# Opened steps: an output product between A11 and A12 instead of behind both

## The chip, the cores and the metric

The kernel runs on one core of one Trainium2 chip. The metric is the device time of one launch in microseconds (us); less is better. Times of several runs are given as their median.

The engines go by the names that the profile uses: PE is TensorE (PEld its weight loads, which overlap its matmuls), DVE is VectorE, ACT is ScalarE, POOL is GpSimd, SP is the queue that issues most transfers. PSUM is the memory that matmuls write to, in banks of 512 fp32 columns for each of 128 partitions.

## What is computed

Two blocks in a row, all in fp32: a filter in the frequency domain along the sequence, and then an MLP with SiLU on every token.

```python
# x (8, 3008, 256); filt_r, filt_i (1505, 256)
X = np.fft.rfft(x, axis=1)
Y = X * (filt_r + 1j * filt_i)[None]
y = np.fft.irfft(Y, n=3008, axis=1).astype(np.float32)
# w_in (256, 2048); w_out (2048, 256); 24064 tokens
h = y.reshape(24064, 256) @ w_in
g = h * (1.0 / (1.0 + np.exp(-h)))
out = g @ w_out
```

## The kernel before

**The MLP as a run of steps.** The 3008 tokens of a batch are taken as two halves of the channel-major tile `y`, and each half in three pieces, so that a batch has six "pairs" (a pair is two token blocks of 256, or of 240 in the last piece of a half). The 2048 hidden channels are eight blocks of 2 x 128. A step is one pair with one such block, so a batch has 48 steps (`STEPS`) and the kernel 384. In each step the 2 x 2 block product with w_in is done with seven products instead of eight (combinations of weights named A11, A12, S3, A22, S1, S2, S4 and sums of tokens in `ty`), and the product with w_out likewise, with seven output products.

**`hidden(step)`, line 719**, computes the hidden half of a step. It is a generator; between two `yield`s lies one round, and there are eight rounds. Two PSUM banks take its products: `px` (tag `x`) for A11, S2, S3 and A22, which accumulate on each other, and `pyz` (tag `yz`), whose first 256 columns are `yo` (S1, S4) and whose second 256 are `zo` (A12). In order:

- round 0: A11 into `px`; ScalarE copies it to `sums[:, 0]` (line 740)
- round 1: A12 into `zo`; VectorE adds the copy to it and writes g0 (line 743); then `finish()` lets VectorE do the last two sums of the step before, g6 and g7 (lines 770 and 771)
- round 2: S2 onto `px`; ScalarE copies it (747) and applies SiLU to g0
- round 3: S1 into `yo`
- round 4: S3 onto `px`; ScalarE copies it (753), VectorE adds it to `yo` for g2 (754)
- round 5: nothing
- round 6: A22 onto `px`; ScalarE takes SiLU from it (g3), then SiLU of g2
- round 7: S4 onto `yo`; VectorE's sum g1 (762), SiLU of it, and the sums g4 and g5 (764)

**`project(step)`, line 778**, is the other generator: the seven output products of a step, one to a round, each reading one of g0 to g7 and adding to one of four accumulator banks. In the order of `PROJECT` (line 775) they read g0, g3, g2, g4, g5, g6, g7; at the first step of a pair the order is another. Here they are called p1 to p7. `LAG` is 1: while `hidden(step)` runs, `project(step - 1)` runs.

**The loop, line 1141,** interleaves the two by hand: every engine executes its instructions in the order in which they are written out here. In each of `ROUNDS` = 8 rounds it lets `hidden` and then `project` go on by one, and then `until` writes out whatever is due from the plan (`pending`): the pieces of the Fourier stages for the next batches, the token sums of the next pair, the output's transposes and stores.

**Opened steps.** Some pieces of the Fourier stages have to borrow the banks `x` and `yz`, which only stand free between two steps. Where such pieces are planned, `open_step` (line 658) puts the step into the set `opened` and plans the pieces 0.06 of a step ahead of it. In an opened step the loop first writes out two output products (line 1149 to 1151), then the borrowed pieces (line 1152), then the eight rounds. Since two output products are used up, `project` has five left and is held back in two rounds (line 1154). `plan(b, ...)` opens three steps for each batch b from 2 on and two for batch 1, counted from the batch's first step:

- 44 steps ahead (not for batch 1): `stage1` of rows 6, with its two results in `x` and `yz`, evicted by ScalarE (`x`) and VectorE (`yz`), and then `stage1` of rows 7 in banks of its own
- 36 steps ahead: `stage3` of the batch before in `x` and `yz`, evicted by VectorE (`x`) and ScalarE (`yz`), and then `forward` of group 0 in banks of its own
- 10 steps ahead: `stage3` of groups 0 (in `x` and `yz`) and 1 (own banks); in this step's round 1 the token sums of a later pair (`tokens`, line 709) are also written out, three operations of VectorE

Of the kernel before, what the change touches and what calls it, by code (L numbers as in the profile page):

```python
# [167 lines left out]
def kernel(  # L168
# [421 lines left out]
    joined, opened = set(), set()  # L590
# [176 lines left out]
    def finish():  # L767

        for g, n in unfinished:
            combine(v, g[:, 6, 0:n], g[:, 2, 0:n], g[:, 4, 0:n], ALU.subtract)  # L770
            combine(v, g[:, 7, 0:n], g[:, 3, 0:n], g[:, 6, 0:n], ALU.subtract)
        unfinished.clear()
# [5 lines left out]
    def project(step):  # L778

        pair, jp = divmod(step, NJP)  # L780
        n, g = pairs[pair][3], g_t.pop(step)
        if jp == 0:
            acc[pair] = {}
        last = jp == NJP - 1

        order = PROJECT
        if jp == 0 and step in joined:
            order = PROJECT[0:2] + PROJECT[3:5] + PROJECT[2:3] + PROJECT[5:]
        elif jp == 0:
            order = PROJECT[2:3] + PROJECT[0:2] + PROJECT[3:]  # L790
        for c, k, i, h in order:
            if i not in acc[pair]:
                acc[pair][i] = accps.tile([128, 2, 256], FP32, name=f"acc_{pair}_{i}", tag=f"a{i}")

            nc.tensor.matmul(out=acc[pair][i][:, h, 0:n], lhsT=w_t[:, jp, c, 1], rhs=g[:, k, 0:n],  # L795
                             start=(jp == 0 and h == 0), stop=last, skip_group_check=True)
            if last and (h == 1 or i == 3):
                drain(pair, i)
            yield
# [327 lines left out]
    for pair in range(len(pairs)):  # L1127
        step, rnd = combines[pair % per] if pair != 1 else (7, 5)
        pending.append((pair // per * STEPS + step + rnd / ROUNDS, 98, lambda pair=pair: tokens(pair)))
        for chunk in range(2 if pair < len(pairs) - 1 else 0):  # L1130
            step, rnd = stores[pair % per][chunk]
# [4 lines left out]
    def until(time):  # L1136
        while pending and pending[0][0] <= time:
            pending.pop(0)[2]()

    until(-1e-3)  # L1140
    for step in range(n_steps + LAG):
        work = []
        if step < n_steps:
            work.append(hidden(step))
        else:
            finish()
        if step >= LAG:
            work.append(project(step - LAG))
        if step in opened:
            for _ in range(2):  # L1150
                next(work[1])
        until(step - 0.05)
        for rnd in range(ROUNDS):
            held = work[1:] if step in opened and rnd in (0, 2) else []
            work = [w for w in work if w in held or next(w, work) is not work]
            until(step + rnd / ROUNDS)
        assert not work
# [30 lines left out]
```

## Time and profile before

| what | value |
|---|---|
| median of 3 runs | 2586.41 us (2585.56 to 2587.24) |
| profiled execution | 2588.03 us, of which the span from first to last instruction 2586.3 us |
| granted TensorE clock | 0.995 |
| output products (L795), matmuls | 5376, 1508.7 us busy, 375 ns each |
| products into `px` from `ty` (L732) | 2304, 678.1 us busy, 376 ns each |
| products into `pyz` from `y` (L732) | 1536, 454.2 us busy, 377 ns each |
| VectorE sums out of `pyz` (L703) | 1152, 479.7 us busy, 416 ns each |

The page's busy times are unions by group: two matmuls overlap in the pipeline, so one that is shown with 375 ns starts 0.215 us after the one before it. Every fp32 product is two such matmuls (x2 in a row of the timeline), so a product of 256 tokens takes 0.43 us of TensorE. All sums of VectorE, whatever the line that asks for them, carry the line of their helper `combine`, L703; they are told apart by their tiles: `g<-pyz,abc` is a sum out of the bank, `g<-g` one of the others, `ty<-y` a token sum.

In rows of the order of time the first number is the start in us from the start of the span, the second the length; x2 means that two instructions of one kind were merged; brackets give the idle time of the engine ahead of the row and the instruction that ended it. A row of waits has the waiting instruction, the one that it waited for, the sum in us, how often, and the longest.

### The profile page before, as it was taken

The page shows a single profiled execution, that of the slowest core. Times are in us where ns is not written, and L with a number is a line of the kernel's source. Part 1 is how long each engine was busy: PE and PEld are TensorE (multiplying, and loading weights), DVE is VectorE, ACT ScalarE, POOL GpSimd, SP SyncE. Part 2 cuts the span into 40 slices and gives each one's busy share as a digit, 9 for nine tenths or more (in the row PEclk, how much of TensorE's full clock was granted, in tenths as well). Part 3 has the DMA queues.
Part 4 walks back from the last instruction along what each step waited for, and adds up shares of the span by engine and source line. Part 5 has one row for each costly group of instructions (what it writes and reads, how often), then busy time and mean ns, then how long its engine had stood idle before and what let it go on. Part 6 is the DMA issues. An engine that isn't in the chain of part 4 may idle for free.

```text
span 2586.3 us, 48366 instructions
## 1 busy us (share of the span) xinstructions
PE 2560.6 (99%) x18972; PEld 2198.1 (85%) x18972; DVE 1681.0 (65%) x3569; ACT 1113.9 (43%) x3014; POOL 424.9 (16%) x672
## 2 busy tenths in 40 slices
PE   8999999999999999999999999999999999999998
PEld 6688888888888888888888888888888888888987
DVE  7766666666666766666666666666666676555554
ACT  3544444444444444444444444444444444444443
POOL 2211211121112111211122111211121112101101
PEclk9899999999999999999999999999999999999999
DMA  8431232212222222231223222331232211210000
GB/s 276 142 90 45 68 83 67 60 53 82 63 63 64 71 65 58 70 78 59 68 51 89 58 66 58 79 76 52 64 74 67 73 45 27 65 20 16 9 17 17
DMA packets 200077, 171.08 MB, mean 66 GB/s; under 512 B 122116, under 2 KB 174196, under 8 KB 199060
## 3 DMA queue, kind: packets, MB, share of 16 engines
q1 hardware_dynamic: 178520, 117.04, 19.0%
q0 software_dynamic: 16928, 44.65, 5.4%
q10 hardware_dynamic: 4400, 6.29, 0.8%
q8 instruction: 149, 2.44, 0.4%
q14 instruction: 80, 0.66, 0.1%
HBM read 96.05 MB, written 81.26 MB: 69 GB/s over the span
## 4 chain that ended last, share of the span: by engine, by line
PE 95%; DVE 2%; DMA 1%; ACT 1%; issue 0%; ACTq 0%; SPq 0%; DVEq 0%
PE acc L795 43%; PE px L732 25%; PE pyz L732 19%; PE pd L560 3%; PE pb L446 2%; PE pc L489 2%; PE pf L416 1%; DMA w_t<-in_x_dram 0%; DVE g L703 0%; PE pa L342 0%; DMA filt<-in_filt_r_dram 0%; DMA d_t<-d_tbl 0%; PE pa L333 0%; DMA raw<-in_moe_w_out_dram 0%; ACT t L349 0%
## 5 line engine op out<-in xcount | busy, mean ns | idle before, releaser
L795 PE MATMUL acc<-g,w_t 128*128 128x256 f32 (+1 forms) x5376 | 1508.7, 375 | 0.4 <-DVE g L703 0.4
L795 PEld LDWEIGHTS acc<-g,w_t 128*128 128x128 f32 x5376 | 1021.3, 190 | 115.6 <-DVE g L703 0.8
L703 DVE TENSOR_TENSOR g<-pyz,abc 128x256 f32<-128x256 f32 (+1 forms) x1152 | 479.7, 416 | 614.9 <-ACT abc L753 360.1
L703 DVE TENSOR_TENSOR g<-g 128x256 f32<-128x256 f32 (+3 forms) x1152 | 599.3, 520 | 196.9 <-ACT g L736 183.7
L732 PE MATMUL px<-ty,w_t 128*128 128x256 f32 (+1 forms) x2304 | 678.1, 376 | 0.5 <-ACT abc L753 0.5
L736 ACT ACTIVATE g<-g 128x256 f32<-128x256 f32 (+1 forms) x1152 | 472.9, 410 | 250.1 <-DVE g L703 250.1
L703 POOL TENSOR_TENSOR s<-s 128x256 f32<-128x256 f32 (+1 forms) x329 | 255.1, 793 | 1412.7 <-DVE s L815 1307.6
L732 PEld LDWEIGHTS px<-ty,w_t 128*128 128x128 f32 x2304 | 432.3, 190 | 64.5 <-issue 8.2
L732 PE MATMUL pyz<-y,w_t 128*128 128x256 f32 (+1 forms) x1536 | 454.2, 377 | 0.0
L732 PEld LDWEIGHTS pyz<-y,w_t 128*128 128x128 f32 x1536 | 283.4, 189 | 48.3 <-DVE g L703 8.6
L747 ACT COPY abc<-px 128x256 f32<-128x256 f32 (+1 forms) x384 | 141.5, 368 | 364.6 <-PE px L732 364.6
L753 ACT COPY abc<-px 128x256 f32<-128x256 f32 (+1 forms) x384 | 141.9, 370 | 336.1 <-PE px L732 335.3
L736 ACT ACTIVATE g<-px 128x256 f32<-128x256 f32 (+1 forms) x384 | 146.1, 381 | 297.3 <-PE px L732 297.2
L732 PE MATMUL px<-y,w_t 128*128 128x256 f32 (+1 forms) x768 | 232.2, 384 | 2.0 <-ACT y L246 1.0
L732 PE MATMUL pyz<-ty,w_t 128*128 128x256 f32 (+1 forms) x768 | 225.7, 376 | 0.2 <-DVE g L703 0.2
L732 PEld LDWEIGHTS px<-y,w_t 128*128 128x128 f32 x768 | 140.3, 189 | 34.9 <-DVE y L582 5.8
L732 PEld LDWEIGHTS pyz<-ty,w_t 128*128 128x128 f32 x768 | 144.5, 190 | 18.8 <-DVE g L703 1.0
L740 ACT COPY abc<-px 128x256 f32<-128x256 f32 (+1 forms) x384 | 135.8, 354 | 45.0 <-PE px L732 45.0
L560 PEld LDWEIGHTS pd<-wi_t,t 48*64 48x64 f32 x4096 | 67.2, 138 | 30.9 <-ACT g L736 16.4
L560 PE MATMUL pd<-wi_t,t 48*64 48x47 f32 x4096 | 73.5, 236 | 5.7 <-issue 3.5
L428 POOL DMA_DIRECT2D d<-tf x144 | 71.7, 505 | 31.3 <-DVE tf L424 27.3
L815 ACT COPY s<-acc 128x512 f32<-128x512 f32 (+1 forms) x94 | 54.3, 578 | 47.5 <-PE acc L795 47.4
(118 smaller groups left out, 1312.7 us busy)
## 6 DMA issues: line engine op xcount, KB each, us to landing
t<-d SPq DMA_DIRECT2D x120, 192.0 KB
d<-q POOLq DMA_DIRECT2D x86, 256.0 KB, 2.6
t<-d SPq DMA_DIRECT2D x84, 256.0 KB
out_dram<-o SPq DMA_DIRECT2D x636, 32.0 KB
d<-tf POOLq DMA_DIRECT2D x144, 96.0 KB, 3.5
xr<-in_x_dram SPq DMA_DIRECT2D x6, 1472.0 KB
x_all<-in_x_dram SPq DMA_DIRECT2D x72, 96.0 KB
x_all<-xr SPq DMA_DIRECT2D x72, 96.0 KB
```

What stands on the lines that cost most here:

```text
L428: nc.gpsimd.dma_start(out=d1[k // 2, :, k % 2, n0:n0 + 4], in_=us["tf"][32 * k:32 * k + NS].rearrange("p q n c -> p (q n) c"))
L446: nc.tensor.matmul(out=ps[k][32 * j:32 * j + 32, ri, :], lhsT=d_t[rows, 4 * g + at, ri, :], rhs=t2[rows, at, :], start=True, stop=True)
L489: nc.tensor.matmul(out=ps[j][64 * k:64 * k + 64, a, :], lhsT=e_t[rows, g + a, k, ri, :], rhs=zs[k][rows, ri, :], start=(a == 0 and ri == 0 ...
L560: nc.tensor.matmul(out=ps[h][c0:c0 + 64, cb, i, :], lhsT=t4s[g][rows, i, 128 * cb + c0:128 * cb + c0 + 64], rhs=wi_t[rows, :], start=True, ...
L703: eng.tensor_tensor(out=out, in0=in0, in1=in1, op=op)
L732: nc.tensor.matmul(out=out, lhsT=w_t[:, jp, c, 0], rhs=rhs, start=start, stop=True, skip_group_check=True)
L736: nc.scalar.activation(out=g[:, k, 0:n], in_=g[:, k, 0:n] if src is None else src, func=AFT.Silu)
L740: nc.scalar.copy(out=sums[:, 0, 0:n], in_=xo)
L747: nc.scalar.copy(out=sums[:, 1, 0:n], in_=xo)
L753: nc.scalar.copy(out=sums[:, 2, 0:n], in_=xo)
L795: nc.tensor.matmul(out=acc[pair][i][:, h, 0:n], lhsT=w_t[:, jp, c, 1], rhs=g[:, k, 0:n], start=(jp == 0 and h == 0), stop=last, skip_group ...
L815: copy(out=s[:, 2 * i:2 * i + 2, 0:n], in_=acc[pair][i][:, :, 0:n])
```

## The change

One line of the loop. In an opened step `project` is held in rounds 1 and 2 and no longer in rounds 0 and 2:

```diff
         until(step - 0.05)
         for rnd in range(ROUNDS):
-            held = work[1:] if step in opened and rnd in (0, 2) else []
+            held = work[1:] if step in opened and rnd in (1, 2) else []
             work = [w for w in work if w in held or next(w, work) is not work]
             until(step + rnd / ROUNDS)
```

The order of products in an opened step, after p1, p2 and the borrowed pieces:

```
before: A11 A12 p3  S2 S1 p4 S3 p5 p6 A22 p7 S4
after:  A11 p3  A12 S2 S1 p4 S3 p5 p6 A22 p7 S4
```

With A12 its sum g0 and the sums of `finish()` are written out one product later. The other 364 steps are as they were.

## The prediction

> **What bounds the kernel now.** I read the page's busy shares first, then the chain of waits, then the waits of the weight loads, then the order of time in single steps. Products are named by the weight combination that they use: a step computes A11, A12, S2, S1, S3, A22, S4 (w_in), and the output products p1 to p7 of the step before stand among them.
>
> The page's busy row and the first line of its chain:
> ```profile
> PE 2560.6 (99%) x18972; PEld 2198.1 (85%) x18972; DVE 1681.0 (65%) x3569; ACT 1113.9 (43%) x3014; POOL 424.9 (16%) x672
> ...
> PE 95%; DVE 2%; DMA 1%; ACT 1%; issue 0%; ACTq 0%; SPq 0%; DVEq 0%
> ```
> TensorE is the bound: a moment in which it stands still in the main loop lengthens the span by as much, and the other engines matter only as far as a product waits for them. So the question is what waits the new order makes.
>
> From the waits of the weight loads:
> ```profile
> PEld pyz L732 <- DVE g L703: 9.7, 34, 0.6
> ```
> Products of the pyz bank already wait 34 times, 9.7 us in all, for VectorE sums that read that bank. Such a wait is the one to look for.
>
> One opened step, engine by engine (start, length; a stage-3 and a forward block stand before it, and its p1 and p2 before those). TensorE:
> ```profile
> 489.65 0.70 PE L732 MATMUL px<-y,w_t 128*128 128x256 f32 x2
> 490.18 0.59 PE L732 MATMUL pyz<-y,w_t 128*128 128x256 f32 x2
> 490.61 0.59 PE L795 MATMUL acc<-g,w_t 128*128 128x256 f32 x2
> 491.05 0.59 PE L732 MATMUL px<-ty,w_t 128*128 128x256 f32 x2
> 491.48 0.59 PE L732 MATMUL pyz<-ty,w_t 128*128 128x256 f32 x2
> ```
> VectorE in the same stretch:
> ```profile
> 490.88 0.42 DVE L703 TENSOR_TENSOR g<-pyz,abc 128x256 f32<-128x256 f32 x1 [1.31 <-ACT abc L740]
> 491.22 0.87 DVE L703 TENSOR_TENSOR g<-g 128x256 f32<-128x256 f32 x2
> ```
> And the weight loads of S1 and p4:
> ```profile
> 491.36 0.31 PEld L732 LDWEIGHTS pyz<-ty,w_t 128*128 128x128 f32 x2
> 491.69 0.41 PEld L795 LDWEIGHTS acc<-g,w_t 128*128 128x128 f32 x2
> ```
> The matmul rows are A11, A12, p3, S2, S1: one product each 0.43 us (490.18, 490.61, 491.05, 491.48). Only A11 to A12 takes 0.53, as TensorE restarts after the block. The first VectorE row is g0, the sum at line 743 that reads A12's half of the pyz bank. S1's weight load starts at 491.36, 0.06 after g0 ends (490.88 + 0.42 = 491.30), and S1 writes the other half of that bank. The other two kinds of opened step show the same: g0 ends 438.30 and S1's load starts 438.35; 348.45 and 348.51. Three equal distances: I take it that S1 waits for g0. Now it costs nothing: S1's matmul still starts 0.43 after S2's.
>
> An ordinary step with a product between A11 and A12, for the time from A12 to g0:
> ```profile
> 469.32 0.59 PE L732 MATMUL pyz<-y,w_t 128*128 128x256 f32 x2
> ...
> 470.02 0.42 DVE L703 TENSOR_TENSOR g<-pyz,abc 128x256 f32<-128x256 f32 x1 [0.75 <-PE pyz L732]
> ```
> g0 starts 0.70 after A12's first matmul (0.11 after the modelled end) and ends at 470.44. There S1 comes four products after A12 (471.05), so nothing shows.
>
> VectorE's work in the kind of opened step that carries a pair's token differences:
> ```profile
> 348.03 0.42 DVE L703 TENSOR_TENSOR g<-pyz,abc 128x256 f32<-128x256 f32 x1 [1.28 <-ACT abc L740]
> 348.37 0.88 DVE L703 TENSOR_TENSOR g<-g 128x256 f32<-128x256 f32 x2
> 349.17 0.65 DVE L703 TENSOR_TENSOR ty<-y 128x480 f32<-128x480 f32 x1
> 349.85 0.85 DVE L703 TENSOR_TENSOR ty<-y,ty 128x240 f32<-128x240 f32 x2
> 350.62 0.80 DVE L582 COPY y<-pd 128x376 f32<-128x376 f32 x1
> 351.26 0.42 DVE L703 TENSOR_TENSOR g<-pyz,abc 128x256 f32<-128x256 f32 x1
> ```
> The weight load of S4 there:
> ```profile
> 351.73 0.30 PEld L732 LDWEIGHTS pyz<-y,w_t 128*128 128x128 f32 x2 [0.31 <-DVE g L703]
> ```
> From g0 on VectorE is not idle for 3.6 us; S4 then waits 0.31 for the last sum. So whatever delays g0 also delays S4.
>
> **What the Trainium skill says.** "PSUM — Partial Sum Buffer", section "PSUM bank collisions raise a hardware error": access by two engines has to be kept apart by bank and quadrant, not by address; disjoint columns of one bank still collide. That is why S1 (columns 0 to 255 of the bank) must stay behind a sum that reads columns 256 to 511, and the 0.05 to 0.06 us in three steps agree. Same page, "Engine vs sequencer instructions": matmuls start in program order and VectorE's queue is first in, first out; so p4 and all behind it wait with S1, and everything behind g0 moves with g0. The trace agrees: p4's load is the next after S1's. "Perfetto Trace Analysis", "Tensor Engine Instruction (MATMUL, LD_WEIGHTS)": the shown end of a matmul is an estimate and its semaphore comes later; the 0.11 us from A12's end to g0 is that, so I use start-to-start times.
>
> **The change part by part.** Opened steps are counted from the plan: batch 1 has two (36 and 10 steps ahead of the batch), batches 2 to 7 have three (44, 36, 10), 2 + 6 x 3 = 20 of 384. All have 256 tokens, and the step projected in them is never a pair's first, so p3 is always S4 with g2.
>
> Removed and added instructions: none. No DMA, no copy and no issue on SP's or POOL's queue is moved; two products change places on TensorE, and with A12 its sum g0 and the two sums of the unfinished step (line 769) come later on VectorE.
>
> *p3 earlier by one place.* It reads g2, whose Silu ended before the block (433.42 to 433.83 in the step whose A11 starts at 436.64). Cost 0, gain 0, because TensorE is kept busy either way.
>
> *A11 to S2.* Between them stand two products as before, so ScalarE's copy of A11 (490.44 to 490.81) stays hidden: 0.
>
> *A12 later by one place.* Its matmul starts at 490.61 and not 490.18. Could that take away a wait of A12 for its bank? Its bank's eviction by ScalarE ended at 489.61, before A11; the 0.53 is the restart and is paid by whichever product follows A11. Bounds: 0 to -0.10 a step; I take 0.
>
> *g0 and S1.* Before, g0 started with the later of ScalarE's copy (490.81) and A12. Now A12 decides: 490.61 + 0.70 = 491.31, end 491.73, S1's load 491.79, its matmul 0.12 later at 491.91, where it was 491.48. TensorE stands for 0.43 us, since only S2 is left between A12 and S1. Queued behind S1 are p4, S3, p5, p6, A22, p7 and S4, and ScalarE's copy of S3 and the sum g2 wait for S3: the rest of the step moves as a whole. Bounds: counting from g0's start in the three kinds (0.43 to 0.45 later) gives at most 0.45; counting to the matmul after S1 (a product that follows an idle restart starts 0.54 after the load, as A12 after A11: 491.79 + 0.54 = 492.33, where p4 was 491.91) gives 0.42. I take 0.43, ends 0.41 and 0.45.
>
> *What follows.* The unfinished sums end 0.43 later, and p6 needs the first of them (g6): g0's end + 0.44. S1's load + four products (1.7 us) is where p6 loads. No wait. ScalarE's Silu of g0 starts at 491.95, behind the copy of S2 (from 491.68), and g0's new end, 491.73, is ahead of that: 0. In the seven steps 10 ahead of a batch VectorE's row is 0.43 later as a whole, but S4 is 0.43 later too, so the 0.31 stays 0.31 and isn't paid twice.
>
> Sum: 20 x 0.43 = 8.6 us (8.2 to 9.0). Against the profiled execution: 2588.03 us (span 2586.3 and 1.7 around it) becomes 2596.6. That execution lies 1.6 above the median of the runs, 2586.41, to which the same sum gives 2595.0.
>
> **The rivals.**
> *S1 doesn't wait for g0.* Then the 0.06 is chance, and only the seven token steps lose, as g0's delay reaches S4: 7 x 0.43 = 3.0 us, 2589.4. For it: the two halves are different data. Against: three equal distances, and the bank rule. Chance 0.06.
>
> *The stall is absorbed (the other side: not slower).* Later in the loop TensorE waits anyway, for example at the pyz loads (9.7 us in all). If those waits end on work that the delay doesn't touch, the 0.43 is taken out of them; it decides from the point where the waits in the two steps after reach 0.43. With all of it absorbed and A12's restart gain of up to 0.10: 2586.4 down to 2584.4. For it: VectorE is idle 35% of the span. Against: no weight load in two of the three kinds waits in the rest of its step, and in the third the wait begins with g0 itself. Chance 0.05.
>
> *The token steps pay twice.* If S4's wait grows by the delay on top of S1's: 8.6 + 7 x 0.43 = 11.6 us, 2598.0. For it: VectorE's unbroken row. Against: both ends of that wait move alike. Chance 0.07.
>
> **How the numbers follow.** My forecast has 0.82: 2595.0. What can be told from no change is about 0.2%, 5.2 us. Slower: 0.82 + 0.07 = 0.89. Within: 0.06 + 0.03 of the absorbed case = 0.09. Faster 0.02. The range is the forecast's 8.2 to 9.0 with some 2 us for medians of few runs below, and up to the double payment: 2592.0 to 2598.2; 0.11 lies below it.
>
> **What would show it.** In the changed kernel the weight load of S1 in the 20 opened steps carries a wait for VectorE's g, some 0.5 us from the end of S2's load; the row "pyz waits for g" grows from 34 times to about 54, and from 9.7 by about 10 us. g0 starts 0.70 after A12 and names PE as releaser, not ScalarE. S4's 0.31 in the token steps stays. I am wrong if S1's load comes ahead of g0's end, or if the steps after an opened one lose waits that they have now.

## The result and the profile after

| | median | runs | ratio to before (95% interval) |
|---|---|---|---|
| before | 2586.74 us | 6 | |
| after | 2595.76 us | 6 | 1.0036 (1.0023 to 1.0048) |

The change makes the kernel slower: the ratio is 1.0036, and the medians lie 9.0 us apart. The profiled executions have spans of 2586.3 and 2594.4 us.

The busy row and the first row of the chain, of the changed kernel:

```profile
PE 2564.0 (99%) x18972; PEld 2196.5 (85%) x18972; DVE 1682.0 (65%) x3569; ACT 1113.2 (43%) x3014; POOL 424.0 (16%) x672
...
PE 94%; DVE 3%; DMA 1%; ACT 1%; issue 1%; POOL 0%; DVEq 0%; SPq 0%; ACTq 0%; POOLq 0%
```

The instruction counts are those of before. In the chain VectorE's share has gone from 2 to 3% and TensorE's from 95 to 94% (rounded; the whole loss is under 0.4%): there are more places where TensorE stands until VectorE lets it go on. The waits of the weight loads say which (the pyz row had 9.7 us in 34 waits before):

```profile
PEld pyz L732 <- DVE g L703: 21.6, 59, 0.6
```

The opened step that the prediction took apart, in the changed kernel; it starts 1.03 us later now. TensorE's matmuls are A11, p3, A12, S2, S1:

```profile
490.68 0.70 PE L732 MATMUL px<-y,w_t 128*128 128x256 f32 x2
491.22 0.59 PE L795 MATMUL acc<-g,w_t 128*128 128x256 f32 x2
491.65 0.59 PE L732 MATMUL pyz<-y,w_t 128*128 128x256 f32 x2
492.08 0.59 PE L732 MATMUL px<-ty,w_t 128*128 128x256 f32 x2
492.83 0.70 PE L732 MATMUL pyz<-ty,w_t 128*128 128x256 f32 x2 [0.15 <-DVE g L703]
```

VectorE, from g0 on:

```profile
492.35 0.42 DVE L703 TENSOR_TENSOR g<-pyz,abc 128x256 f32<-128x256 f32 x1 [1.74 <-PE pyz L732]
492.69 0.87 DVE L703 TENSOR_TENSOR g<-g 128x256 f32<-128x256 f32 x2
```

And the weight loads of S2 and S1:

```profile
491.89 0.38 PEld L732 LDWEIGHTS px<-ty,w_t 128*128 128x128 f32 x2
492.83 0.30 PEld L732 LDWEIGHTS pyz<-ty,w_t 128*128 128x128 f32 x2 [0.56 <-DVE g L703]
```

g0 starts 0.70 after A12 and names TensorE as what it waited for, where it had named ScalarE's copy. (In the kernel before it also started 0.70 after A12, 490.18 to 490.88, though the view names the copy there.) It ends at 492.77, and S1's load starts 0.06 later, after an idle time that the view now puts down to VectorE's g. From A11 to S1's load it is 2.15 us; before it was 1.72. The matmul row names only 0.15 us of idle time, since the modelled end of S2 reaches far into the gap. The loss is read better from the loads, or from the starts: S1's matmul starts 0.75 after S2's, where it was 0.43, and the product behind it another 0.54 later, where it was 0.43. The first gives 0.32 us, the second 0.11.

In a token step (an opened step with the token sums, 10 steps ahead of a batch) S4 waits as before (0.31 then):

```profile
352.34 0.30 PEld L732 LDWEIGHTS pyz<-y,w_t 128*128 128x128 f32 x2 [0.33 <-DVE g L703]
```

The whole loss can be read without modelled ends, from A11 of one opened step to A11 of the next. These are starts of A11's weight load in the order of time, subtracted, for one batch; each stretch belongs to the opened step at its head. Of all 19 stretches 17 are longer by 0.41 to 0.45 us. The other two, behind the token steps at 659 and 1286 us in the kernel before, differ by -0.04 and +0.57. Each holds a long wait of TensorE in or just behind a stage-3 block that varies from profile to profile: 1.06 us at 681 us became 0.57 (put down to no instruction), and 0.96 us at 1307 us became 1.09 (for the block's eviction).

| kernel | from the token step (10 ahead) | from the step 44 ahead | from the step 36 ahead |
|---|---|---|---|
| before | 89.82 | 53.00 | 169.72 |
| after | 90.26 | 53.43 | 170.14 |
| after less before | 0.44 | 0.43 | 0.42 |

The same starts taken from one step to the next leave those waits out. From A11 of an opened step to A11 of the step behind it, each of the 20 is longer by 0.42 to 0.45 us, 8.5 us in all; of the other steps only three differ by more than 0.06 us (the very first, and the two with the waits just named). So every opened step costs 0.42 to 0.45 us, whatever pieces it has borrowed the banks for, and the sum lies inside the interval of the measured ratio (6 to 12 us).

### The profile page after: what moved, and what is told of

It reads as the page before. It is cut to its first block, busy times and chain, and to the rows that moved or that the text cites. A ratio compares the mean times of both kernels' runs of the same rounds, so it can differ in the third digit from the quotient of the medians.

```text
span 2594.4 us, 48366 instructions
## 1 busy us (share of the span) xinstructions
PE 2564.0 (99%) x18972; PEld 2196.5 (85%) x18972; DVE 1682.0 (65%) x3569; ACT 1113.2 (43%) x3014; POOL 424.0 (16%) x672
## 4 chain that ended last, share of the span: by engine, by line
PE 94%; DVE 3%; DMA 1%; ACT 1%; issue 1%; POOL 0%; DVEq 0%; SPq 0%; ACTq 0%; POOLq 0%
PE acc L795 43%; PE px L732 25%; PE pyz L732 19%; PE pd L560 3%; PE pb L446 2%; PE pc L489 2%; DVE g L703 1%; PE pf L416 1%; DMA x_all<-in_x_dram 1%; DVE w_t L302 1%; PE pa L342 0%; DMA raw<-in_moe_w_out_dram 0%; DVE w_t L703 0%; ACT t L349 0%; DVE p L468 0%
```

## The experiments

The theory is that of the prediction: S1 writes the bank from which VectorE reads g0, so it waits for that read; with A12 one product later only S2 is left to hide it. The rivals are that a late A12 costs by itself, that the wait is for something else, and that part of the cost lies in VectorE's long row in the token steps. All times are medians, beside runs of the kernel before on the same chip: 2586.12 us for the first four, 2585.45 us for the last two.

### A12 late, S1 a product later

```diff
-            held = work[1:] if step in opened and rnd in (0, 2) else []
+            held = work[1:] if step in opened and rnd in (1, 3) else []
```

> Opened steps run A11 p3 A12 S2 p4 S1 S3: A12 is as late as in the changed kernel, but two products (S2 and p4) stand between A12 and S1 again. Theory (S1 waits for g0, the reader of its bank): no wait of S1 in any of the 20 steps; g0 starts 0.43 us later than before, which only reaches S4 in the seven token steps, where its wait grows from 0.31 to about 0.74: 7 x 0.43 = 3.0 us over the kernel before, ratio 1.0012. Rival (a late A12 is what costs, wherever S1 stands): as the changed kernel, about 9 us, ratio 1.0035.

Measured: 2588.96 us, ratio 1.0011 (1.0004 to 1.0018); the rival's 1.0035 is outside. The weight loads from S2 to S1 in the step of 36 ahead (rows: S2, p4, S1), and g0 there:

```profile
490.54 0.38 PEld L732 LDWEIGHTS px<-ty,w_t 128*128 128x128 f32 x2
490.94 0.41 PEld L795 LDWEIGHTS acc<-g,w_t 128*128 128x128 f32 x2
491.47 0.31 PEld L732 LDWEIGHTS pyz<-ty,w_t 128*128 128x128 f32 x2
```
```profile
490.99 0.42 DVE L703 TENSOR_TENSOR g<-pyz,abc 128x256 f32<-128x256 f32 x1 [1.73 <-PE pyz L732]
```

g0 is as late as after the change, and S1's load still starts 0.06 behind its end (491.41). But p4 has filled the time, and nothing is lost. S4 of the token step pays in its place:

```profile
351.42 0.30 PEld L732 LDWEIGHTS pyz<-y,w_t 128*128 128x128 f32 x2 [0.73 <-DVE g L703]
```

The 0.31 has become 0.73. By stretches: 90.25, 53.00, 169.72. Only the token steps lose, 0.43 to 0.44 each from step to step; the other 13 opened steps run as before with a late A12. What counts is the distance from A12 to S1.

### Nothing reads the bank

```diff
-            held = work[1:] if step in opened and rnd in (0, 2) else []
+            held = work[1:] if step in opened and rnd in (1, 2) else []
...
-        combine(v, g[:, 0, 0:n], zo, sums[:, 0, 0:n], ALU.add)
+        combine(v, g[:, 0, 0:n], sums[:, 0, 0:n] if step in opened else zo, sums[:, 0, 0:n], ALU.add)
```

> The changed order, but in the 20 opened steps the sum g0 reads ScalarE's copy twice and not A12's half of the bank (left out: A12's product in g0 of these steps), so that nothing reads the bank between A12 and S1. Theory: S1 no longer waits, g0 starts with ScalarE's copy as before, S4's 0.31 in the token steps stays: time of the kernel before, ratio 1.0000 within 0.0007. Rival (the place of A12 or p3 on TensorE itself costs, or the wait is for something other than the read): about 8 to 9 us, ratio 1.0033.

Measured: 2584.95 us, ratio 0.9997 (0.9989 to 1.0005); the rival's 1.0033 is outside. This kernel leaves A12's product out of g0 in the opened steps, and nothing else. The changed order, with the same products in the same places, costs nothing when g0 doesn't read A12's half. g0, and the loads of S2 and S1:

```profile
487.94 0.43 DVE L703 TENSOR_TENSOR g<-abc 128x256 f32<-128x256 f32 x1 [1.26 <-ACT abc L740]
```
```profile
487.96 0.38 PEld L732 LDWEIGHTS px<-ty,w_t 128*128 128x128 f32 x2
488.36 0.41 PEld L732 LDWEIGHTS pyz<-ty,w_t 128*128 128x128 f32 x2
```

S1's load starts 0.02 after S2's ends, and just before g0 (487.94 to 488.37) has ended; g0 itself no longer waits for A12. In the six steps 44 ahead of a batch g0 ends 0.05 before S1's load, so the times alone could not tell a wait from chance there. The instructions in the traces can: in the kernel before and in the changed one S1's load carries a wait for the semaphore that VectorE's sums count up, in all 384 steps; in this kernel it carries none in the 20 opened steps, and still does in the other 364. Stretches: 89.80, 53.01, 169.71, the kernel before.

### The bank is read twice, in the order of before

```diff
-        combine(v, g[:, 0, 0:n], zo, sums[:, 0, 0:n], ALU.add)
+        for _ in range(2 if step in opened else 1):
+            combine(v, g[:, 0, 0:n], zo, sums[:, 0, 0:n], ALU.add)
```

> The order of before, but in the 20 opened steps VectorE makes the sum g0 twice, one after the other, so that the bank is read 0.34 to 0.42 us longer (start to start of two such sums, and the length of one). Theory: S1, which stood just behind g0 without losing time, now waits 0.34 to 0.42: 20 x 0.34 to 0.42 = 6.8 to 8.4 us, ratio 1.0026 to 1.0032. Rival (S1 doesn't wait for the read; only VectorE's longer row in the token steps reaches S4): 7 x 0.34 = 2.4 us, ratio 1.0009.

Measured: 2594.62 us, ratio 1.0033 (1.0020 to 1.0045); the rival's 1.0009 is outside. A12 stands where it stood before and S1 stalls all the same. The two sums, and S1's load:

```profile
491.40 0.89 DVE L703 TENSOR_TENSOR g<-pyz,abc 128x256 f32<-128x256 f32 x2 [1.31 <-ACT abc L740]
```
```profile
492.34 0.30 PEld L732 LDWEIGHTS pyz<-ty,w_t 128*128 128x128 f32 x2 [0.58 <-DVE g L703]
```

The second read ends at 492.29, S1's load starts 0.05 later. The stretches are 90.27, 53.46 and 170.15, that is 0.43 to 0.46 more than before. The expectation had 0.34 to 0.42 for the second sum; it starts 0.46 after the first, more than was reckoned, and each opened step loses 0.45 to 0.48 from step to step.

### The token sums a step later

S4's wait in the token step is in the kernel before as well, and A12 of the step behind it waits too, for the sum that reads what S4 wrote. In the kernel before:

```profile
353.26 0.30 PEld L732 LDWEIGHTS pyz<-y,w_t 128*128 128x128 f32 x2 [0.37 <-DVE g L703]
```

The token sums aren't needed until step 40, and VectorE has idle time in step 39.

```diff
-    combines = ((-2, 1), (6, 1), (11, 5), (22, 5), (26, 6), (38, 1))
+    combines = ((-2, 1), (6, 1), (11, 5), (22, 5), (26, 6), (39, 1))
```

> The order of before; the three token sums of the fifth pair are written out one step later (round 1 of step 39 and not of step 38), so that the opened step 10 ahead of a batch has no token sums. Theory: S4's wait of 0.31 there and A12's of 0.37 in the next step (six of the seven) go, which cost 0.17 and 0.24 us in the row of matmuls: 7 x 0.17 + 6 x 0.24 = 2.6 us less than before, ratio 0.9990. Rival (the three sums make the same wait in step 39 as VectorE is late there): no change or up to 3 us more, ratio 1.0000 to 1.0012.

Measured: 2583.46 us, ratio 0.9989 (0.9982 to 0.9995), faster than both kernels. The token sums in step 39 on VectorE, with the next sum out of the bank behind them:

```profile
353.96 0.65 DVE L703 TENSOR_TENSOR ty<-y 128x480 f32<-128x480 f32 x1
354.65 0.85 DVE L703 TENSOR_TENSOR ty<-y,ty 128x240 f32<-128x240 f32 x2
355.61 0.42 DVE L703 TENSOR_TENSOR g<-pyz,abc 128x256 f32<-128x256 f32 x1
```

And in the token step S4's load, and A12's of the step behind it, which no longer wait:

```profile
350.47 0.41 PEld L732 LDWEIGHTS pyz<-y,w_t 128*128 128x128 f32 x2
```
```profile
351.80 0.38 PEld L732 LDWEIGHTS pyz<-y,w_t 128*128 128x128 f32 x2
```

The token sums end at 355.50, 0.11 ahead of that next sum, so they delay nothing. The stretch behind the token step is 89.41, 0.41 less than before, and the others are unchanged. The two parts come out as expected: the token step is shorter by 0.16 to 0.18, and in six of the seven cases the step behind it by 0.24.

### Both together

The next two kernels have the token sums in step 39 and another order of the opened steps: held in rounds 1 and 2 (the change), or in rounds 1 and 3 (A12 late, two products before S1).

```diff
-    combines = ((-2, 1), (6, 1), (11, 5), (22, 5), (26, 6), (38, 1))
+    combines = ((-2, 1), (6, 1), (11, 5), (22, 5), (26, 6), (39, 1))
...
-            held = work[1:] if step in opened and rnd in (0, 2) else []
+            held = work[1:] if step in opened and rnd in (1, 2) else []
```

> The token sums moved to step 39 and the changed order of the opened steps together. Theory: S1's wait has nothing to do with the token sums, so all 20 steps lose the same 0.42 us (8.4) on top of what moving the sums gave (ratio 0.9989): ratio 1.0022, and no wait of S4. Rival (part of the change's cost came from VectorE's long row in the seven token steps): 13 x 0.42 = 5.5 us on top, ratio 1.0010.

Measured: 2591.56 us, ratio 1.0024 (1.0014 to 1.0034); the rival's 1.0010 is outside. Stretches: 89.83, 53.43, 170.12, which is 0.42, 0.43 and 0.41 more than with the token sums moved alone. The token steps lose to S1 like all others, and no more than these.

The other kernel has `(1, 3)` in the last line.

> The token sums moved to step 39, and in the opened steps A11 p3 A12 S2 p4 S1 S3. Theory: with two products between A12 and S1 and no long row of VectorE behind g0, a late A12 costs nothing: as with the token sums moved alone, ratio 0.9989. Rival (the 3 us that this order cost came from A12's place and not from S4 behind the token sums): ratio 1.0000.

Measured: 2583.59 us, ratio 0.9993 (0.9985 to 1.0001). The interval holds both expectations, so the time doesn't decide. The stretches do: 89.41, 53.01, 169.70, those of the token sums moved alone, and S4's wait is gone from the token steps. The waits of pyz loads for VectorE in the kernel with the sums moved alone, and in this one:

```profile
PEld pyz L732 <- DVE g L703: 6.1, 26, 0.6
```
```profile
PEld pyz L732 <- DVE g L703: 5.6, 23, 0.6
```

## Why the prediction was right

**S1 waits for g0.** This was read from three distances of 0.05 to 0.06 us, and could have been chance. It is shown now from three sides: without the read S1 goes ahead (nothing reads the bank), with a longer read it waits although A12 is early (the bank is read twice), and with a product put between it is covered (A12 late, S1 a product later). The wait stands in the program: S1's load carries it, and carries none once g0 doesn't read the bank. The two write and read different columns of one bank, and the Trainium skill ("PSUM — Partial Sum Buffer", "PSUM bank collisions raise a hardware error") asks for a semaphore by bank and quadrant and not by address; that agrees with the trace. But the two halves are also one tile of the program, `pyz`. No run has them in two tiles or in two banks, so it is not shown that the shared bank is the reason and not the shared tile.

**The size.** The forecast was 0.43 us in each of 20 steps, 8.6 us and 2595.0; the steps show 0.42 to 0.45, 8.5 us in all, and the median is 2595.76. The runs of one kernel spread over 4 to 5 us, so the remaining 0.8 us has no cause to be looked for. The term came out well since its parts were all in the profile of before: A12's new place was p3's old one, and the time from A12 to g0 could be taken from ordinary steps that already have a product between A11 and A12.

**p3, A11 to S2, and A12's bank cost nothing.** They had been put at 0. The kernel without the read has all three of these moves and runs as before.

**S4 in the token steps isn't paid twice.** Its wait is 0.33 where it was 0.31, and the token steps lose no more than the others (0.44 against 0.42 and 0.43). When S1 doesn't wait but g0 is late, S4's wait grows by 0.42: the delay is there in either case, and is paid once, by whichever product comes to it first.

**The stall isn't absorbed later.** Behind the opened steps nothing gives it back. One step two places behind an opened one is shorter by 0.49 (the wait at 681 us), but it is shorter by 0.61 in the kernel where nothing reads the bank, in which no opened step loses anything; so that isn't the stall absorbed.

**What was a little off.** The row of pyz waits was to grow by 20 waits and about 10 us; it grew by 25 and about 12. The 20 waits of S1, at 0.54 to 0.56 each, are 11.0 of that. The other five are loads of A12 in steps that aren't opened, with idle times of 0.15 us each, 0.8 in all. They were there before as well, at 0.146 to 0.150, and the shortest that the row holds is 0.151: they crossed the limit of the list and cost nothing new. S4's waits in the token steps make up the rest, 0.2.

The matmul of S1 was to start 0.12 after its load, as in the kernel before. After the idle time it starts with its load (both at 492.83), and the missing 0.11 comes at the product behind it; the second way of counting in the prediction, 0.54 from the load to the product after S1, had this right, and the sum is the same. And g6 was put at 0.44 after the end of g0; in the profile of before it ends 0.33 after it. That makes p6 safer still.

## What to carry to other kernels

When two products are exchanged, don't count only the products. Look at what each of them releases, and how many products stand between the one that fills a bank and the next one that writes any part of it: an order written by hand may have just as many as the reader of the bank needs, as this one had, and the profile shows it as a load that starts a few hundredths behind that reader with no idle time named. The list of waits didn't show it here: S1's load had stood idle for only 0.11 to 0.13 us. Such a wait is the first thing to price in a reordering. Where the loss per place is small, measure it between the starts of one instruction in successive periods, which shows hundredths of a microsecond when the medians of whole runs spread over several.

## What the runs showed that was not expected

Two sums of VectorE that write the same output follow each other at 0.46 us start to start (the bank is read twice), where g0 and the next sum, into another part of the tile, are 0.34 apart (490.88 and 491.22 in the kernel before). The shared output isn't needed for this: g7, which reads g6 and writes elsewhere, starts 0.45 after g6. In both cases the later sum carries a wait for VectorE's own semaphore and starts 0.03 after the sum ahead of it has ended, while g6, which needs nothing from g0, starts 0.08 before g0 has ended. A sum that has to wait for the one just ahead so starts 0.11 to 0.12 us later here than one that hasn't.

A weight load may be late by some 0.1 us at no cost, in this case. S1's load starts 1.72 after A11's in the kernel before and 1.62 where nothing reads the bank, and its matmul starts 0.43 behind S2's in both. The load of the kernel before is already late, but not late enough to move the matmul.
